# Gate logits in four column groups, turned back and added, in a fused attention, FFN and routed-experts kernel

## The chip, the cores and the metric

The kernel runs on one NeuronCore of a Trainium2 chip. The metric is the device time of one execution in microseconds, the median of three runs. The engines are TensorE (PE in the rows; PEld is its weight load, which runs beside the matmuls), VectorE (DVE), ScalarE (ACT), GpSimd (POOL) and SyncE (SP), which issues most transfers.

## The reference, cut to what matters

Three stages follow each other: clustered attention, a dense ELU feed-forward network, and a routed layer of eight experts. The change is in the routing of the third, for 1536 tokens of 512 numbers:

```python
skip_score = x @ w_skip
do_compute = skip_score > 0
xc = x[do_compute]
logits = xc @ w_gate                 # w_gate: 512 x 8
e_idx = np.argmax(logits, axis=1)
probs = softmax(logits); gate_w = probs[arange, e_idx]
for e in range(E):
    mask = e_idx == e
    h = np.maximum(xc[mask] @ w1[e], 0.0)
    y[mask] = gate_w[mask, None] * (h @ w2[e])
out[do_compute] = xc + y
```

## The kernel before

The tokens are two blocks of 768, each of six tiles of 128 tokens. The FFN runs over each block in 16 k-steps, one for each 128 of the hidden units. A k-step computes the hidden products of part 0 (three token tiles) into PSUM bank p and those of part 1 into bank v (`ffn_h`, L1275), passes each through the ELU (`ffn_elu`, L1295 to L1303: two ScalarE steps, a VectorE step, a ScalarE step and a VectorE step that all work on that bank or its copy), and then issues the 18 second products of the step before (`ffn_second`, L1314), which add into the other PSUM banks. All engines follow the program order in this stage.

Routing of a tile of 128 tokens has these steps. `turn` (T): four transposes into a bank (L1451) and a ScalarE copy of it to `x2T` (L1453). `logits` (L): four matmuls into a bank, each with 128 columns of `x2T` stationary and 16 columns of the gate table `wgs` moving (L1459; the 16 are eight gates, the skip weight and zeros), and a VectorE copy of the 128x16 result to `lg` (L1461). After the last tile of a half, `choose` (C, L1465 to L1478) finds each token's expert on VectorE and cumulates the counts in `cum`; `rank` (R) turns those into places with two small matmuls (L1482, L1483) and builds selections (L1486); `fill` (F) writes tokens and gate weights to slots (matmuls L1500, adds L1504).

Block 0 is routed beside the FFN of block 1. `route_beside` is a generator that `ffn` advances twice in each k-step: once after half of the second products (first slot) and once after the other half (second slot). Its order for each half of three tiles is T, L, T, L, T, L, one in each slot, then choose, an empty slot, rank, two empty slots, fill. Its banks come from one cycle over both halves:

```python
tags = itertools.cycle(("p", "v"))
halves = [self.route(b, 3 * half, y[half], lambda: self.ps(next(tags))[:, 0, :]) for half in range(2)]
```

Each call gives the next of the two banks; the tile that had the bank before must have been read.

Block 1 is routed in the tail, after its last k-step (`route_last`). TensorE's order there is the list `TAIL`, written out by hand. An h step is three of the second products that were held back (`h3` for tile 3, and so on); after the last of them for a tile that tile is copied out. `x-` and `x0` to `x5` gather the tokens of expert 0 with selections (L1537, matmuls L1541). `N5` (`ranks`, L1619) counts the tokens of each expert and gives the number of the next expert, with which its weights are fetched. The other engines' order in the tail is set by the scheduler, from the emitted program. The groups of the tail are tiles 0 to 2, 3 to 4, and 5 alone. Its banks rotate in the list `free`, which begins as p and v, loses v at `x-` and gains two more when the held products of tiles 4 and 5 are done.

Of the kernel before, what the change touches and what calls it, by code (L numbers as in the profile page):

```python
# [31 lines left out]
HOLD = 4  # L32


TAIL = ("h3 h3 h3 T0 T2 h3 L0 T1 h5 L2 L1 T3 h5 C0 h4 h4 R0 h4 h4 x- T4 h5 L3 L4 C3 h5 x0 T5 R3 x2 L5 x4 F0 C5 R5 N5 x3 x1 x5 F5 F3").split()

LATER = 8

# [125 lines left out]
class _Core:  # L164
# [75 lines left out]
    def constants(self):  # L240
        nc, c, E = self.nc, self.const, self.E
        V, S, G = nc.vector, nc.scalar, nc.gpsimd
        self.x2_d = self.dram.tile([self.NT, self.DM], F32, name="x2_d")
        self.wf_d = self.dram.tile([self.DFF // 128, 128, 1024], F32, name="wf_d")
        self.inv_d = self.dram.tile([self.B * self.H // 2, 12, 128], F32, name="inv_d")

        self.RS = (self.NT - min(WIDTHS) + 127) // 128 * 128
        self.meta_d = self.dram.tile([E * self.RS, 2], I32, name="meta_d")

        self.ones16 = c.tile([128, 128], BF16, name="ones16")  # L250
        V.memset(self.ones16, 1.0)
        self.tri16 = c.tile([128, 128], BF16, name="tri16")
        G.affine_select(out=self.tri16, in_=self.ones16, pattern=[[1, 128]], compare_op=ALU.is_gt,
                        fill=0.0, base=0, channel_multiplier=-1)

        io = c.tile([128, 16], I32, name="io")
        G.iota(io, pattern=[[1, 16]], base=0, channel_multiplier=0)
        self.iota16 = c.tile([128, 16], F32, name="iota16")
        V.tensor_copy(self.iota16, io)
        self.iota_neg = c.tile([128, 16], F32, name="iota_neg")  # L260
        V.tensor_scalar(self.iota_neg, self.iota16, -16.0, None, ALU.add)
        self.ebase = c.tile([128, E], F32, name="ebase")
        V.tensor_scalar(self.ebase, self.iota16[:, 0:E], float(self.RS), None, ALU.mult)
        self.tokid = c.tile([128, self.B, self.NC], I32, name="tokid")
        G.iota(self.tokid, pattern=[[self.S, self.B], [1, self.NC]], base=0, channel_multiplier=self.NC)
        io = self.pre.tile([128, CAP], I32, name="io_slot")
        G.iota(io, pattern=[[1, CAP]], base=0, channel_multiplier=0)
        self.iota_slot = c.tile([128, CAP], F32, name="iota_slot")
        V.tensor_copy(self.iota_slot, io)

        self.tok_neg = c.tile([128, self.B * self.NC], F32, name="tok_neg")
        V.tensor_scalar(self.tok_neg, self.tokid.rearrange("p b c -> p (b c)"), -NOWHERE, None, ALU.add)

        NTL = self.B * self.NC
        self.oh = c.tile([128, NTL, E], BF16, name="oh")
        self.pos = c.tile([128, NTL], F32, name="pos")
        self.gate = c.tile([128, NTL], F32, name="gate")

        self.slots = c.tile([SLOT, 2, E, 2], F32, name="slots")
        V.memset(self.slots, 0.0)  # L280

        self.oh_sc = c.tile([64, 2], F32, name="oh_sc")
        V.memset(self.oh_sc[0:32, 0:1], 1.0)
        V.memset(self.oh_sc[0:32, 1:2], 0.0)
        V.memset(self.oh_sc[32:64, 0:1], MASKED)
        V.memset(self.oh_sc[32:64, 1:2], -MASKED)
        self.sort_constants()
        self.top2 = c.tile([128, 1], I32, name="top2")
        V.memset(self.top2, -(1 << 30))

        self.acc = c.tile([128, E], BF16, name="acc")
        V.memset(self.acc, 0.0)


        self.wgs = c.tile([128, self.DM // 128, 16], F32, name="wgs")
        V.memset(self.wgs, 0.0)
        nc.sync.dma_start(out=self.wgs[:, :, 0:E], in_=self.w_gate.rearrange("(c p) e -> p c e", p=128))
        nc.sync.dma_start(out=self.wgs[:, :, E:E + 1], in_=self.w_skip.rearrange("(c p o) -> p c o", p=128, o=1))
# [732 lines left out]
    def redo_experts(self, d):  # L1031
# [9 lines left out]
        for i in range(T):  # L1041
            ps = self.ps("p")[:, 0, :]
            for c in range(4):
                PE.transpose(ps[:, c * 128:c * 128 + 128], out[:, i, c * 128:c * 128 + 128], self.ident)
            V.tensor_copy(xT[:, :, i * 128:i * 128 + 128], ps.rearrange("p (c n) -> p c n", c=4))
            ps = self.ps("v")[:, 0, 0:16]
            for c in range(4):
                PE.matmul(ps, lhsT=xT[:, c, i * 128:i * 128 + 128], rhs=self.wgs[:, c, :], start=(c == 0), stop=(c == 3))
            V.tensor_copy(lg[:, i], ps)
        ex, eq = t("ex", [128, T, E]), t("eq", [128, T, E])  # L1050
        V.tensor_reduce(st[:, 0], lg[:, :, 0:E], axis=AX.X, op=ALU.max)
# [271 lines left out]
    def second_ops(self, k):  # L1323

        NF = self.DFF // 128
        bl, f = divmod(k, NF)
        (w2H, w2L), g = self.w_sp[k, 1], [self.gs[k, part] for part in range(2)]

        def product(part, t, i):
            a, w = ((g[part][0], w2H), (g[part][1], w2H), (g[part][0], w2L))[i]  # L1330
            self.nc.tensor.matmul(self.y[bl][part][t], lhsT=a[:, t * 128:t * 128 + 128], rhs=w,  # L1331
                                  start=(f == 0 and i == 0), stop=(f == NF - 1 and i == 2))
        return product

# [85 lines left out]
    def route(self, b, c0, y, bank):  # L1420
# [32 lines left out]
            S.copy(held[t], ps)  # L1453

        def logits(t):
            lp = bank()[:, 0:16]
            x2T = held.pop(t)
            for j in range(4):
                PE.matmul(lp, lhsT=x2T[:, j * 128:j * 128 + 128], rhs=self.wgs[:, j, :],  # L1459
                          start=(j == 0), stop=(j == 3))  # L1460
            V.tensor_copy(lg[:, t, :], lp)  # L1461

        def choose():
            lge = lg[:, :, 0:E]
# [29 lines left out]
        def fill():  # L1494
# [7 lines left out]
            for g, n in enumerate((SLOT, CAP - SLOT)):  # L1502
                flat = self.slots[0:n, g].rearrange("p e v -> p (e v)")
                V.tensor_tensor(flat, ps[0:n, g * 2 * E:(g + 1) * 2 * E], flat, ALU.add)  # L1504
        return ([lambda t=t: copy(t) for t in range(nt)], [lambda t=t: turn(t) for t in range(nt)],
                [lambda t=t: logits(t) for t in range(nt)], choose, rank, fill)

    def first_fetch(self):

# [40 lines left out]
    def route_beside(self, b, y):  # L1550

        tags = itertools.cycle(("p", "v"))
        halves = [self.route(b, 3 * half, y[half], lambda: self.ps(next(tags))[:, 0, :]) for half in range(2)]
        for h in halves:
            for op in h[0]:
                op()
        yield
        for _, turn, logits, choose, rank, fill in halves:
            for i in range(3):
                turn[i]()  # L1560
                yield
                logits[i]()
                yield
            choose()
            yield
            yield
            rank()
            yield
            yield
            yield  # L1570
            fill()
            yield
        yield from self.first_fetch()

    def route_last(self, b, y, rest):

        self.oh0 = self.dp.tile([128, self.NC], F32, name="oh0")
        free, steps = ["p", "v"], {}

        def bank():  # L1580
            free.append(free.pop(0))
            return self.ps(free[-1])[:, 0, :]
        for c0, ys in ((0, y[0]), (3, y[1][0:2]), (5, y[1][2:3])):
            copy, turn, logits, choose, rank, fill = self.route(b, c0, ys, bank)
            for i in range(len(ys)):
                steps["c", c0 + i], steps["T", c0 + i], steps["L", c0 + i] = copy[i], turn[i], logits[i]
            steps["C", c0], steps["R", c0], steps["F", c0] = choose, rank, fill
        steps["N", 5] = lambda: self.ranks(bank)
        for c in range(3):
            steps["c", c]()  # L1590
        held = {c: [op for t, op in rest if t == c - 3] for c in range(3, 6)}
        with self.tc.manual_schedule(engines={mybir.EngineType.PE}):
            for what in TAIL:
                if what[0] == "h":
                    c = int(what[1])
                    held[c].pop(0)()
                    if not held[c]:
                        steps["c", c]()
                        if c > 3:
                            free.append(("sB", "t1")[c - 4])  # L1600
                elif what == "x-":
                    a = self.ps("sA")
                    self.xs_ps = [x[:, 0:WIDTHS[0]] for x in (a[:, 0, :], a[:, 1, :], self.ps("t0")[:, 0, :], self.ps("v")[:, 0, :])]
                    self.first_x(None)
                    free.remove("v")
                elif what[0] == "x":
                    self.first_x(int(what[1]))
                else:
                    steps[what[0], int(what[1])]()
        self.xs = {0: self.first_split()}  # L1610
# [366 lines left out]
```

## Time and profile before

| | us |
|---|---|
| median of 3 runs | 756.83 (756.13 to 759.34) |
| profiled execution | 756.85 |
| its span, first to last instruction | 755.1 |
| TensorE busy | 633.5 (84%) |
| VectorE busy | 429.9 (57%) |
| ScalarE busy | 392.4 (52%) |
| GpSimd busy | 272.8 (36%) |

TensorE is the busiest engine. Its busy time counts overlapping passes once, and the ends of matmuls are modelled, so the start-to-start distances of a timeline say more than the durations. An idle time in brackets in a timeline row stands before that row, with what ended it.

### The profile page before, as it was taken

The page shows a single profiled execution, that of the slowest core. Times are in us where ns is not written, and L with a number is a line of the kernel's source. Part 1 is how long each engine was busy: PE and PEld are TensorE (multiplying, and loading weights), DVE is VectorE, ACT ScalarE, POOL GpSimd, SP SyncE. Part 2 cuts the span into 40 slices and gives each one's busy share as a digit, 9 for nine tenths or more (in the row PEclk, how much of TensorE's full clock was granted, in tenths as well). Part 3 has the DMA queues.
Part 4 walks back from the last instruction along what each step waited for, and adds up shares of the span by engine and source line. Part 5 has one row for each costly group of instructions (what it writes and reads, how often), then busy time and mean ns, then how long its engine had stood idle before and what let it go on. Part 6 is the DMA issues. An engine that isn't in the chain of part 4 may idle for free.

```text
span 755.1 us, 11501 instructions
## 1 busy us (share of the span) xinstructions
PE 633.5 (84%) x3940; PEld 564.4 (75%) x3940; DVE 429.9 (57%) x978; ACT 392.4 (52%) x848; POOL 272.8 (36%) x289
## 2 busy tenths in 40 slices
PE   4882871984671399999999999999999998999996
PEld 2761761863561299978989888899998897999995
DVE  5681771883561298899788775243244554135663
ACT  3761750863640289776777765544444532124552
POOL 3237066047147302765664352323222203121101
PEclk9795795897695599999999999999999999999999
DMA  7867064566331029656655452642411037979960
GB/s 178 202 156 200 10 147 115 133 141 179 96 87 37 24 78 245 191 180 204 205 179 153 163 165 95 250 168 79 158 52 48 15 149 246 375 257 322 339 228 18
DMA packets 99958, 118.30 MB, mean 157 GB/s; under 512 B 47554, under 2 KB 68210, under 8 KB 99889
## 3 DMA queue, kind: packets, MB, share of 16 engines
q1 hardware_dynamic: 92080, 106.70, 46.4%
q0 software_dynamic: 6096, 10.34, 4.3%
q8 instruction: 33, 0.54, 0.3%
q10 hardware_dynamic: 1712, 0.43, 0.3%
q14 instruction: 37, 0.30, 0.1%
HBM read 80.17 MB, written 27.80 MB: 143 GB/s over the span
## 4 chain that ended last, share of the span: by engine, by line
PE 65%; DVE 13%; issue 10%; ACT 6%; another core or an unknown queue 5%; DMA 1%; ACTq 0%; POOL 0%; POOLq 0%; DVEq 0%
PE ps_p L1275 7%; PE ps_v L1275 6%; PE ps_t L1726 5%; PE ps_v L1741 4%; PE ps_p L1741 4%; PE ps_t L513 4%; PE ps_sB L1314 3%; PE ps_sA L1314 3%; PE ps_t L1314 3%; PE ps_v L544 3%; PE ps_sB L492 2%; DVE ptL L531 2%; DVE cv_b L1223 2%; PE ps_sA L1331 2%
## 5 line engine op out<-in xcount | busy, mean ns | idle before, releaser
L513 PE MATMUL ps_t<-ident,pe 128*128 128x128 f32 x288 | 54.1, 309 | 55.3 <-issue 29.9
L525 ACT ACTIVATE ptH<-ps_t 128x384 fp32r<-128x384 f32 x96 | 46.3, 493 | 89.3 <-remote 73.0
L531 DVE TENSOR_TENSOR ptL<-ps_t,ptH 128x384 fp32r<-128x384 f32 x96 | 52.1, 552 | 69.7 <-issue 54.7
L513 PEld LDWEIGHTS ps_t<-ident,pe 128*128 128x128 f32 x288 | 38.5, 158 | 65.8 <-issue 33.2
L874 POOL DMA_INDIRECT og<-od,idx x48 | 51.5, 1073 | 55.6 <-ACT rp L836 29.8
L544 PE MATMUL ps_v<-ptH,vt 128*128 128x256 f32 x144 | 43.4, 324 | 24.9 <-issue 12.4
L1229 POOL TENSOR_TENSOR r<-cv_b,cv_t 128x512 int32<-128x512 int32 x32 | 43.0, 1344 | 47.8 <-DVE cv_b L1223 17.7
L544 PEld LDWEIGHTS ps_v<-ptH,vt 128*128 128x128 f32 x144 | 30.1, 211 | 28.1 <-issue 14.4
L1774 POOL DMA_INDIRECT out_dram<-o,dest x10 | 11.5, 1151 | 96.0 <-DVE o L1772 95.4
L1275 PE MATMUL ps_p<-xH,w1H 128*128 128x384 f32 x128 | 44.3, 346 | 1.9 <-DVE gL L1303 1.4
L1275 PE MATMUL ps_v<-xH,w1H 128*128 128x384 f32 x124 | 42.0, 338 | 1.3 <-DVE gL L1303 1.3
L1299 DVE SCALAR_TENSOR_TENSOR ps_p<-e,ps_p 128x384 f32<-128x384 f32 x32 | 17.9, 561 | 44.0 <-ACT e L1297 44.0
L1275 PE MATMUL ps_p<-xL,w1H 128*128 128x384 f32 x128 | 43.0, 336 | 0.0
L1275 PE MATMUL ps_v<-xL,w1H 128*128 128x384 f32 x124 | 41.6, 335 | 0.0
L544 PE MATMUL ps_v<-ptL,vt 128*128 128x256 f32 x144 | 41.5, 312 | 0.0
L1255 POOL TENSOR_TENSOR w2L<-r,w2H 128x512 fp32r<-128x512 f32 x12 | 15.3, 1277 | 71.2 <-PE ps_t L1314 61.5
L1295 ACT ACTIVATE e<-ps_p 128x384 f32<-128x384 f32 x32 | 15.6, 488 | 40.7 <-PE ps_p L1275 40.5
L1741 PEld LDWEIGHTS ps_v<-xs,ew 128*128 128x128 f32 x256 | 34.6, 195 | 1.9
L1741 PE MATMUL ps_p<-xs,ew 128*128 128x128 f32 (+2 forms) x256 | 35.6, 281 | 0.5 <-ACT xs L1689 0.5
L1741 PE MATMUL ps_v<-xs,ew 128*128 128x128 f32 (+2 forms) x256 | 35.8, 284 | 0.0
L776 POOL DMA_INDIRECT kvs<-rowsH,idx x24 | 23.6, 984 | 33.5 <-DVE idx L754 26.8
L1741 PEld LDWEIGHTS ps_p<-xs,ew 128*128 128x128 f32 x256 | 33.8, 191 | 2.3 <-ACT xs L1689 0.6
(473 smaller groups left out, 1989.7 us busy)
## 6 DMA issues: line engine op xcount, KB each, us to landing
ew<-in_moe_w_dram SPq DMA_DIRECT2D x32, 1024.0 KB
d<-in_moe_w_in_dram SPq DMA_DIRECT2D x16, 512.0 KB
d<-in_moe_w_out_dram SPq DMA_DIRECT2D x16, 512.0 KB
wf_d<-r SPq DMA_DIRECT2D x16, 512.0 KB
r<-wf_d SPq DMA_DIRECT2D x16, 512.0 KB
zk<-kvs SPq DMA_DIRECT2D x8, 520.0 KB
KA<-kH SPq DMA_DIRECT2D x16, 192.0 KB
kvs<-zeros SPq DMA_DIRECT2D x8, 325.0 KB
```

Source lines behind the costliest of these rows:

```text
L513: self.nc.tensor.transpose(ps[:, 0, j * 128:j * 128 + 128], self.pe[u][:, half, j * 128:j * 128 + 128], self.ident)
L525: self.nc.scalar.activation(self.split(u, half)[0], self.tp[u, half][:, 0, 0:384].rearrange("p (c q) -> p c q", c=3), AF.Copy)
L531: self.nc.vector.tensor_tensor(l, self.tp.pop((u, half))[:, 0, 0:384].rearrange("p (c q) -> p c q", c=3), h.bitcast(F32), ALU.subtract)
L544: self.nc.tensor.matmul(self.vp[n, j], lhsT=self.vt[n][:, j // NG, c, :], rhs=t, start=(part == 0 and i == 0), stop=(part == 3 and i == 2 ...
L776: store = self.nc.gpsimd.indirect_dma_start(dst[2 * j + h], bass.IndirectOffsetOnAxis(ap=self.index(j, c, r), axis=0), self.sort_rows(j, c ...
L874: self.nc.gpsimd.indirect_dma_start(self.og[j][:, c, h, :], None, self.o_d[i], bass.IndirectOffsetOnAxis(ap=self.index(j, c, h), axis=0), ...
L1229: G.tensor_tensor(r[:, j * 512:j * 512 + 512].bitcast(I32), b, self.cvt.pop((f, j)), ALU.add)
L1275: self.nc.tensor.matmul(ps, lhsT=w[:, c, :], rhs=x[:, c, :], start=(i == 0), stop=(i == 11))
L1299: V.scalar_tensor_tensor(ps, e, -1.0, ps, ALU.add, ALU.max)
L1314: self.nc.tensor.matmul(self.y[bl][part][t], lhsT=a[:, t * 128:t * 128 + 128], rhs=w, start=(f == 0 and i == 0), stop=(f == NF - 1 and i = ...
L1726: PE.matmul(y[0][0:W], lhsT=a, rhs=b, start=(f == 0 and i == 0), stop=(f == NF - 1 and i == 2))
L1741: PE.matmul(ps[:, 0:W], lhsT=w1[:, c, i * 128:i * 128 + 128], rhs=xs[:, c, 0:W], start=(c == 0), stop=(c == 3))
```

## The change

The gate table is padded to 32 columns and becomes the stationary operand: the four matmuls of a tile write four groups of 32 PSUM partitions, one for each quarter of the 512 features, with 128 tokens moving. VectorE copies the 128x128 result to `lgT`; TensorE transposes that into columns 128 to 255 of a bank, and VectorE adds the four groups into `lg`. The transpose of a tile is issued behind the next tile's matmuls, in the same bank; that of a group's last tile is a step of its own, `back` (B in `TAIL`), which takes a bank. The group of one tile (tile 5) keeps the old form. `TAIL` is re-made, and `second_ops` looks up its operands later.

```diff
-TAIL = ("h3 h3 h3 T0 T2 h3 L0 T1 h5 L2 L1 T3 h5 C0 h4 h4 R0 h4 h4 x- T4 h5 L3 L4 C3 h5 x0 T5 R3 x2 L5 x4 F0 C5 R5 N5 x3 x1 x5 F5 F3").split()
+TAIL = ("h3 h3 h3 T0 T2 h3 L0 T1 h5 L2 h5 L1 T3 h4 B0 C0 h4 h4 R0 h4 x- T4 h5 L3 h5 L4 x0 B3 C3 T5 x2 R3 L5 x4 "
+        "F0 C5 R5 N5 x3 x1 x5 F5 F3").split()
...
-        self.wgs = c.tile([128, self.DM // 128, 16], F32, name="wgs")
+        self.wgs = c.tile([128, self.DM // 128, 32], F32, name="wgs")
...
-        (w2H, w2L), g = self.w_sp[k, 1], [self.gs[k, part] for part in range(2)]
+        w = self.w_sp[k, 1]
 
         def product(part, t, i):
-            a, w = ((g[part][0], w2H), (g[part][1], w2H), (g[part][0], w2L))[i]
-            self.nc.tensor.matmul(self.y[bl][part][t], lhsT=a[:, t * 128:t * 128 + 128], rhs=w,
+            a = self.gs[k, part][i % 2]
+            self.nc.tensor.matmul(self.y[bl][part][t], lhsT=a[:, t * 128:t * 128 + 128], rhs=w[i // 2],
                                   start=(f == 0 and i == 0), stop=(f == NF - 1 and i == 2))
...
         def logits(t):
-            lp = bank()[:, 0:16]
+            lp = bank()
             x2T = held.pop(t)
+            if nt == 1:
+                for j in range(4):
+                    PE.matmul(lp[:, 0:16], lhsT=x2T[:, j * 128:j * 128 + 128], rhs=self.wgs[:, j, 0:16],
+                              start=(j == 0), stop=(j == 3))
+                V.tensor_copy(lg[:, t, :], lp[:, 0:16])
+                return
             for j in range(4):
-                PE.matmul(lp, lhsT=x2T[:, j * 128:j * 128 + 128], rhs=self.wgs[:, j, :],
-                          start=(j == 0), stop=(j == 3))
-            V.tensor_copy(lg[:, t, :], lp)
+                PE.matmul(lp[32 * j:32 * j + 32, 0:128], lhsT=self.wgs[:, j, :], rhs=x2T[:, j * 128:j * 128 + 128],
+                          start=True, stop=True)
+            before = back(lp)
+            lgT = fw.tile([128, 128], F32, tag="lgT", bufs=2, name="lgT")
+            V.tensor_copy(lgT, lp[:, 0:128])
+            held["back"] = t, lgT
+            before()
+
+        def back(ps=None):
+            if "back" not in held:
+                return lambda: None
+            t, lgT = held.pop("back")
+            if ps is None:
+                ps = bank()
+            PE.transpose(ps[:, 128:256], lgT, self.ident)
+            add = lambda: V.tensor_reduce(lg[:, t, :], ps[:, 128:256].rearrange("p (j e) -> p e j", j=4)[:, 0:16, :], axis=AX.X, op=ALU.add)
+            return add
...
         return ([lambda t=t: copy(t) for t in range(nt)], [lambda t=t: turn(t) for t in range(nt)],
-                [lambda t=t: logits(t) for t in range(nt)], choose, rank, fill)
+                [lambda t=t: logits(t) for t in range(nt)], lambda: back()(), choose, rank, fill)
...
-        for _, turn, logits, choose, rank, fill in halves:
+        for _, turn, logits, back, choose, rank, fill in halves:
             for i in range(3):
                 turn[i]()
                 yield
                 logits[i]()
                 yield
+            back()
             choose()
...
+            steps["B", c0] = back
```

## Rows read from the trace of the kernel before

**Rows 1.** Busy time by stretch: stretch, its length, busy us (instructions) of each engine, clock, transfers.

```profile
500.00:590.00 90.00, 90.00 (x490) 81.91 (x489) 37.69 (x92) 43.35 (x87) 25.33 (x21) 1.00 0.23 77
```

**Rows 2.** Timeline around one turn and gate block of block 0: start, us, instruction.

```profile
529.83 0.49 ACT L1295 ACTIVATE e<-ps_v 128x384 f32<-128x384 f32 x1
...
531.72 0.60 PE L1451 MATMUL ps_p<-ident,xL 128*128 128x128 f32 x4
532.03 0.56 DVE L1303 TENSOR_TENSOR gL<-ps_v,gH 128x384 fp32r<-128x384 f32 x1 [0.56 <-ACT gH L1301]
532.08 0.48 PE L1314 MATMUL ps_sB<-w2H,gL 128*128 128x512 f32 x1
...
534.24 0.96 PE L1459 MATMUL ps_v<-wgs,x2T 128*128 128x16 f32 x8
535.05 0.42 PE L1275 MATMUL ps_p<-xH,w1H 128*128 128x384 f32 x1
```

**Rows 3.** Timeline at block 0's first rank and first fill.

```profile
513.88 0.19 PE L1482 MATMUL ps_p<-oh,tri 128*128 128x24 bf16 x1
514.19 0.56 DVE L1303 TENSOR_TENSOR gL<-ps_v,gH 128x384 fp32r<-128x384 f32 x1 [0.56 <-ACT gH L1301]
...
525.35 0.44 PE L1275 MATMUL ps_p<-xH,w1H 128*128 128x384 f32 x1
525.46 0.24 DVE L1504 TENSOR_TENSOR slots<-ps_v,slots 128x16 f32<-128x16 f32 x2 [2.23 <-PE ps_v L1500]
```

**Rows 4.** Timeline of TensorE around blocks in column groups in the sort.

```profile
40.45 0.34 PE L492 MATMUL ps_sA<-KA,QA 128*128 128x384 f32 x1
40.63 0.34 PE L492 MATMUL ps_sA<-KB,QB 80*128 80x384 f32 x1
40.89 0.85 PE L706 MATMUL ps_p<-sT,cwF 128*32 128x384 f32 x8
41.68 0.39 PE L544 MATMUL ps_v<-ptH,vt 128*128 128x256 f32 x1
...
151.54 0.49 PE L392 MATMUL ps_p<-qH,cwF 128*32 128x384 f32 x1
...
151.86 0.49 PE L392 MATMUL ps_p<-qL,cwF 128*32 128x384 f32 x1
```

**Rows 5.** Chain that ended last, in the tail and in expert 0.

```profile
609.03 0.89 PE ps_v L1459 x8
...
631.42 0.89 PE ps_p L1741 x8
```

**Rows 6.** Timeline of the tail.

```profile
609.96 0.17 DVE L1461 COPY lg<-ps_v 128x16 f32<-128x16 f32 x1 [0.72 <-PE ps_v L1459]
...
611.82 0.14 DVE L1478 TENSOR_TENSOR rcum<-rcum,oh 128x8 bf16<-128x8 bf16 x1
...
612.36 0.19 PE L1482 MATMUL ps_v<-oh,tri 128*128 128x24 bf16 x1
...
620.86 0.85 DVE L1537 TENSOR_SCALAR sel<-iota_slot,pos,oh 128x128 f32<-128x128 f32 x3
...
623.80 0.14 DVE L1478 TENSOR_TENSOR acc<-rcum,oh 128x8 bf16<-128x8 bf16 x1
...
623.99 0.17 PE L1619 MATMUL ps_t<-acc,ones 128*128 128x8 bf16 x1 [0.27 <-DVE acc L1478]
...
626.53 0.29 DVE L1547 COPY xs<-ps_sA 128x128 f32<-128x128 f32 x1 [0.15 <-PE ps_sA L1541]
```

**Rows 7.** Idle times of TensorE with the stretches behind them (timeline, busy time by stretch).

```profile
388.97 0.44 PE L1275 MATMUL ps_p<-xH,w1H 128*128 128x384 f32 x1 [1.02 <-DVE gL L1303]
388.00:392.00 4.00, 3.03 (x16) 2.90 (x17) 3.86 (x8) 2.55 (x6) 2.33 (x2) 1.00 0.59 228
638.93 0.49 PE L1726 MATMUL ps_t<-ew2HL,hH 128*128 128x512 f32 x1 [1.70 <-ACT hH L1744]
641.00:643.00 2.00, 2.00 (x8) 1.71 (x8) 0.29 (x1) 0.28 (x1) 0.00 (x0) 0.50 1.04 369
```

More of the change, by code (lines that the diff above doesn't have):

```diff
@@ L1047, in redo_experts @@
             for c in range(4):
-                PE.matmul(ps, lhsT=xT[:, c, i * 128:i * 128 + 128], rhs=self.wgs[:, c, :], start=(c == 0), stop=(c == 3))
+                PE.matmul(ps, lhsT=xT[:, c, i * 128:i * 128 + 128], rhs=self.wgs[:, c, 0:16], start=(c == 0), stop=(c == 3))
             V.tensor_copy(lg[:, i], ps)
@@ L1583, in route_last @@
         for c0, ys in ((0, y[0]), (3, y[1][0:2]), (5, y[1][2:3])):
-            copy, turn, logits, choose, rank, fill = self.route(b, c0, ys, bank)
+            copy, turn, logits, back, choose, rank, fill = self.route(b, c0, ys, bank)
             for i in range(len(ys)):
-                steps["c", c0 + i], steps["T", c0 + i], steps["L", c0 + i] = copy[i], turn[i], logits[i]
+                for x, f in zip("cTL", (copy, turn, logits)):
+                    steps[x, c0 + i] = f[i]
+            steps["B", c0] = back
             steps["C", c0], steps["R", c0], steps["F", c0] = choose, rank, fill
```

## The prediction, on record before the changed kernel ran

> **What bounds the kernel now.** I read the page's first part, then busy time by stretch, then the chain that ended last, then the timeline around every gate block. The profiled execution took 756.85 us (span 755.1) and the median of the three timed runs is 756.83, so a sum made against 756.85 carries over to the median as it is. A measurement of this kernel can tell about 0.5% (3.8 us) from no change.
>
> What counts are the two places of the gate. The first (block 0) lies inside the second FFN block, where TensorE is busy without a gap from 500 to 590 us [rows 1]: what it saves there is won in full, and each wait put into its queue is paid in full. The second (block 1) is the tail of routing, 604 to 628 us, where TensorE follows the written passage order, and the chain is TensorE nearly throughout, except where a rank or the number of the next expert needs a VectorE result.
>
> **The gate block itself.** Before, four matmuls are eight passes with 128 stationary columns. From the first pass to the next instruction of another kind it is 534.24 to 535.05, 0.81 us [rows 2], or 0.89 in the tail where another gate block stands before it [rows 5]. After, there are four column groups of 32. The trace has such blocks already, in the sort's similarities: eight passes of 128x32 with 384 moving columns take 0.85 us in all, and the next instruction starts 0.79 us after the first [rows 4]. In L392, which has the same form twice over, a round of four passes follows the other at 0.32 us [rows 4]. Four passes one after the other at that width would be 0.7 us even at the 0.18 us from start to start of L492, a lighter form, so the four groups of a round do overlap. Two rounds are 0.64 us, so 0.15 us are lost on the way out; on the way in, L492's pass would have given way at 40.63 + 0.18 = 40.81, and the block began at 40.89, so 0.08 us. With 128 columns a round is a third, 0.11 us: 0.08 + 2 x 0.11 + 0.15 = 0.45 us. The transpose back is a quarter of a turn's four, which take 532.08 - 531.72, 0.36 to 0.45 us, so 0.11 us. A block falls from 0.81 to 0.45 us, or to 0.56 us with a transpose: it saves 0.36 or 0.25 us.
>
> These rows give a factor of 1.8 at most. The Trainium skill, page TensorEngine Tiling (Array Packing), section When to Use Tiling, advises this very swap (narrow operand stationary, four column tiles), and its table of speedups names four as the ceiling. By that page a block would be an estimated 0.20 us, eleven blocks would give 6.7 us, the transposes would take back 1.2, and the time would be 751.4 us. The sum here keeps the row's 0.45 us.
>
> **Block 0, first half (tiles 0 to 2).** Three gate blocks save 0.36 + 0.25 + 0.25, the closing transpose costs 0.11: -0.75 us. That transpose stands a slot behind its copy, with half a step of products between, so it waits for nothing.
>
> **Block 0, what moves with it.** In route_beside the banks come from one cycle of p and v. A half takes eight so far (three turns, three gate blocks, rank, fill), so every turn and rank, which stand in the first slot of a k-step, get p, and every gate block and fill, in the second slot, get v. The FFN writes its hidden part 0 to p at the start of a step and part 1 to v behind it, so that pairing is free: at the first slot p has been read, and behind the second slot v isn't needed for a while. The closing back() takes a ninth bank. From there the pairing is reversed: rank of half 0 on v, its fill on p, three turns on v, three gate blocks on p, the closing transpose of half 1 on v. Its rank and fill are in step again.
>
> A first-slot bank on v must wait until ELU part 1 has read v. Its last reader is L1303, ending 532.03 + 0.56 = 532.59, and the turn stands at 531.72 [rows 2]. With 0.05 us from VectorE to TensorE (acc ends 623.94, TensorE goes on at 623.99 [rows 6]) that is a wait of 0.92 us. At the rank it is 514.19 + 0.56 + 0.05 - 513.88 = 0.92 us [rows 3]. The three turns and the closing transpose repeat the pattern: five waits, 4.6 us. Everything behind them on TensorE (the other half of the second products, then the next step) waits too, and nothing later can take it back, since TensorE has no idle time there. The ELU can't come earlier: its first step starts 529.83, as soon as part 1 is there and part 0 has left ScalarE.
>
> A second-slot bank on p must be read before the next step's first product writes p. For fill that is L1504, ending 525.70, plus 0.05, against 525.35: 0.40 us [rows 3]. For a gate block: passes end about 0.50 us after the slot, 0.04 us to VectorE, a 128x128 copy out of PSUM 0.29 us [rows 6], 0.05 us back: 0.88 against 0.81, +0.07 us. With the sum behind the copy (0.2 us, an estimate between the 0.14 us of an add of 8 columns and that copy's 0.29 us [rows 6]) 1.08: +0.27, twice. The trace doesn't show whether the copy must let the transpose into the same bank finish first; that would be 0 to 0.17 us more for each, and I take 0, as the copy can start when the passes are done. Half 1 in all: 4.6 + 0.11 + 0.40 + 0.61 = +5.7 us. Block 0: **+5.0 us**.
>
> **Block 1, the tail.** Five gate blocks are replaced (tile 5 keeps its form): 0.36 + 0.25 + 0.33 before the first rank, 0.36 + 0.33 before the second, less 0.11 each for the closing transposes. Against that stand two longer ways to a rank. Before, choose starts from the copy right behind the last gate block, and the cumulated counts are there 1.83 us after that copy ends (610.13 to 611.96), ahead of TensorE's coming to the rank at 612.36 [rows 6]. After, the way is copy, transpose, sum, choose. The order covers the copy (a turn and an h step), but the sum is ready 0.4 us after the transpose has left TensorE, the counts 1.83 us later, and only two h steps, 1.4 us (0.70 us each in the chain), stand before the rank: a wait of 0.8 us. That is all that was saved up to there. For the second rank the same: about 1.6 us for two tiles, and T5 and x2 before it, 1.3 to 1.4 us: a wait of 0.6 us. Besides, the second rank now stands behind x2 (0.89 us, eight passes of 128 columns as in rows 5), where it stood ahead of it. So the selections for x4, which were finished at 620.86 + 0.85 when x4 began [rows 6], have only L5 as cover: x4 waits 0.4 to 1.0 us, and L5's copy can stand behind the selections on VectorE, with rank 5 and the choice of the next experts (623.99) behind it. I take **+0.7 us**; it is -0.8 us if none of these waits comes, +1.2 us if all do. All h steps are still issued, and the rewritten second_ops issues the same products in the same order: nothing. The wider gate table is a constant of the start, and TensorE's first use of it is hundreds of microseconds later: nothing; without that cover, one somewhat larger memset.
>
> Sum: 756.85 + 5.0 + 0.7 = **762.5 us**, +0.75%. Its own range is 760.3 to 764.5 us.
>
> **Rivals.**
> *The wrong bank costs nothing* (the other side). If ELU part 1 ended 0.9 us before the slot, the five waits would vanish, and with them the reason for slower. Then 2 x -0.75 for block 0, and between -0.8 and +0.7 in the tail: 754 to 756.5 us, down to 751.4 with the ceiling named above. It decides at the end of L1303 against the first slot; the rows have it 0.9 us late. 0.12.
> *Part of the waits is given back.* The reads of p are quicker and the tail keeps its savings: 757.5 to 760 us. 0.12.
> *The clock falls at the new waits.* It was at 0.50, the 1.2 GHz level, in the 2 us from 641 on, behind an idle of 1.70 us, so at least 1 us was lost [rows 7]. Against it: after an idle of 1.02 us in the FFN it stayed at 1.00 [rows 7], and the waits here are 0.9 us. One to five such falls would be +1 to +5, and more if they last longer: 764 to 771 us. 0.08.
> *The groups run one after the other.* Eight passes of 128 columns are 0.89 us [rows 5], so a block would cost 1.2 us instead of 0.56: 767 to 770 us. Rows 4 speak against it. 0.06.
>
> **How the numbers follow.** My forecast has 0.62. The range 756.5 to 767 leaves out most of the first rival (0.10) and the upper part of the last two (0.08). Slower by over 0.5% (above 760.6): 0.60 + 0.08 + 0.06 + 0.02 from the second rival's edge = 0.76. Within 0.5%: 0.19. Faster: 0.05.
>
> **What the profile would show.** Right: in the second half of block 0's gate (520 to 570 us) turns on ps_v that wait about 0.9 us for L1303, and first products on ps_p that wait for a VectorE copy or sum; gate blocks of 128x32 of about 0.45 us; a first rank of the tail that waits for the counts. Wrong: turns still on ps_p, or on ps_v with no idle time before them; a tail from its first turn to expert 0 that is shorter than before; blocks of 0.8 us and more; a clock below 1.00 between 500 and 600 us.

## The result and the profile after

The changed kernel takes 764.28 us (median of 6 runs, 762.31 to 766.75) against 756.53 us for the kernel before, measured beside it: a ratio of 1.0098, with a 95% interval of 1.0073 to 1.0124. By that ratio it is slower by 7.4 us (the medians differ by 7.75); forecast were 762.5 us and a range of 756.5 to 767. A second comparison (after_again, below) gives 1.0086 [1.0061, 1.0112].

The profiled execution after took 764.43 us (span 762.71), 7.58 us more in span than the one of before. Landmarks that both traces have, here the start of TensorE's first turn of each block, the start of the first product of expert 0 and the end, cut the spans into four stages:

```
                                      before    after    difference
start to first turn of block 0        476.53   478.82    +2.29
block 0 (to first turn of the tail)   127.76   133.99    +6.23
tail (to expert 0)                     23.65    24.34    +0.69
expert 0 to the end                   127.19   125.56    -1.63
```

In the first and the last stage nothing was changed but the width of the gate table, and their differences are taken as those of two executions: the last stage took 127.11 us in after_again, the same kernel, and the first 474.35 us in bank_back, which has every edit of the change up to there. What is the change's own is then +6.92 us. The windows of the trace after, for the stretch of [rows 1] and for block 0 and the tail whole (columns as there):

```profile
500.00:590.00 90.00, 84.14 (x463) 72.83 (x462) 34.76 (x89) 39.50 (x79) 25.64 (x20) 1.00 0.25 82
478.82:612.81 133.99, 127.49 (x695) 110.75 (x693) 52.30 (x125) 62.87 (x127) 35.60 (x28) 1.00 0.28 95
612.81:637.15 24.34, 22.89 (x191) 18.10 (x191) 15.10 (x95) 6.23 (x14) 0.00 (x0) 1.00 0.32 131
```

TensorE, busy for all of the 90 us before, is now idle for 5.86 us of them. The clock stays at 1.00. In these 90 us TensorE sits idle nine times, in the places that the forecast named. The timeline at the first rank, at its fill, around one turn and gate block of the second half, and at a gate block that carries a transpose (it answers to [rows 2, 3]):

```profile
516.02 0.56 DVE L1304 TENSOR_TENSOR gL<-ps_v,gH 128x384 fp32r<-128x384 f32 x1 [0.56 <-ACT gH L1302]
516.63 0.17 PE L1503 MATMUL ps_v<-oh,tri 128*128 128x24 bf16 x1 [0.76 <-DVE gL L1304]
...
528.18 0.24 DVE L1525 TENSOR_TENSOR slots<-ps_p,slots 128x16 f32<-128x16 f32 x2 [2.24 <-PE ps_p L1521]
528.57 0.41 PE L1276 MATMUL ps_p<-xH,w1H 128*128 128x384 f32 x1 [0.43 <-DVE slots L1525]
...
535.24 0.56 DVE L1304 TENSOR_TENSOR gL<-ps_v,gH 128x384 fp32r<-128x384 f32 x1 [0.56 <-ACT gH L1302]
535.85 0.66 PE L1452 MATMUL ps_v<-ident,xL 128*128 128x128 f32 x4 [0.76 <-DVE gL L1304]
...
538.50 0.43 PE L1466 MATMUL ps_p<-x2T,wgs 128*32 128x128 f32 x8
538.99 0.29 DVE L1470 COPY lgT<-ps_p 128x128 f32<-128x128 f32 x1 [3.19 <-PE ps_p L1466]
539.34 0.44 PE L1276 MATMUL ps_p<-xH,w1H 128*128 128x384 f32 x1 [0.41 <-DVE lgT L1470]
...
549.26 0.43 PE L1466 MATMUL ps_p<-x2T,wgs 128*32 128x128 f32 x8
549.62 0.33 PE L1480 MATMUL ps_p<-ident,lgT 128*128 128x128 f32 x1
549.99 0.29 DVE L1470 COPY lgT<-ps_p 128x128 f32<-128x128 f32 x1 [3.42 <-PE ps_p L1480]
550.20 0.22 DVE L1481 TENSOR_REDUCE lg<-ps_p 128x16 f32<-128x64 f32 x1
550.56 0.41 PE L1276 MATMUL ps_p<-xH,w1H 128*128 128x384 f32 x1 [0.61 <-DVE lg L1481]
```

How to read it: the rank, the turns and the closing transpose are now on ps_v and start 0.05 us after the end of L1304, the last reader of that bank. The 0.76 us in brackets is counted from the modelled end of the matmul ahead; from where the instruction would have started it is 0.92 us, since the pass ahead, started at 515.48, gives way after 0.23, at 515.71. There are five such waits (the others at 535.85, 546.62, 557.84 and 569.05), and four first products on ps_p that wait for a VectorE copy, sum or add (528.57, 539.34, 550.56, 561.78). The last group shows what the second kind hangs on: the copy waits for the transpose into the same bank, and the next product for the sum behind the copy.

The gate block itself, in the first half where its bank is v and nothing waits, and the tail's waits (they answer to [rows 2] and [rows 6]):

```profile
481.42 0.43 PE L1466 MATMUL ps_v<-x2T,wgs 128*32 128x128 f32 x8
481.77 0.44 PE L1276 MATMUL ps_p<-xH,w1H 128*128 128x384 f32 x1
...
621.19 0.19 PE L1503 MATMUL ps_p<-oh,tri 128*128 128x24 bf16 x1 [0.22 <-DVE oh L1493]
621.63 0.17 PE L1504 MATMUL ps_p<-rcum,ones 128*128 128x24 bf16 x1 [0.25 <-DVE rcum L1499]
...
628.43 0.39 PE L1562 MATMUL ps_v<-sel,xH 128*128 128x128 f32 x2
629.05 0.18 PE L1503 MATMUL ps_p<-oh,tri 128*128 128x16 bf16 x1 [0.24 <-DVE oh L1493]
629.26 0.17 PE L1504 MATMUL ps_p<-rcum,ones 128*128 128x16 bf16 x1
629.29 1.04 PE L1461 MATMUL ps_sB<-wgs,x2T 128*128 128x16 f32 x8
630.71 0.71 PE L1562 MATMUL ps_sA<-sel,xL 128*128 128x128 f32 x4 [0.37 <-DVE sel L1558]
...
633.20 0.17 PE L1643 MATMUL ps_sB<-acc,ones 128*128 128x8 bf16 x1 [0.33 <-DVE acc L1499]
```

The block is 0.35 us from its first pass to the next product, and about 0.09 us goes ahead of it (the pass before started at 481.10 and a pass of that kind gives way after 0.23): 0.44 us where it was 0.81, as costed. The brackets of the tail's rows, too, count from modelled ends; what these waits cost from start to start is worked out further down.

### The profile page after: what moved, and what is told of

Same layout as the page of the kernel before. It is cut to its first block, busy times and chain, and to the rows that moved or that the text cites. A ratio compares the mean times of both kernels' runs of the same rounds, so it can differ in the third digit from the quotient of the medians.

```text
span 762.7 us, 11532 instructions
## 1 busy us (share of the span) xinstructions
PE 630.3 (83%) x3951; PEld 554.7 (73%) x3951; DVE 432.8 (57%) x989; ACT 391.8 (51%) x848; POOL 272.1 (36%) x289
## 4 chain that ended last, share of the span: by engine, by line
PE 55%; DVE 16%; ACT 9%; another core or an unknown queue 9%; issue 6%; DMA 4%; POOL 0%; SPq 0%; ACTq 0%; POOLq 0%; DVEq 0%
PE ps_p L1276 5%; PE ps_t L1750 4%; PE ps_v L1765 4%; PE ps_p L1765 4%; PE ps_v L1276 4%; PE ps_t L514 3%; PE ps_v L545 3%; PE ps_t L1315 2%; DMA r<-wf_d 2%; PE ps_sB L1315 2%; PE ps_sA L1315 2%; DVE ptL L532 2%; DVE cv_b L1224 2%; ACT pe L506 2%
```

## The experiments

The theory: the closing transpose takes a ninth bank, this reverses the pairing of slots and banks for the rest of block 0, and the waits behind that are the loss; column groups alone are a gain of about half a block each. The first rival: the loss lies in the column groups, their transposes and sums, whatever the bank. The second: it lies in the re-made tail. Two numbers are read from each profile: the block-0 stretch (first turn to first turn of the tail; 127.76 before, 133.99 after) and the tail up to N5, the count that gives the next expert (19.70 before, 20.39 after). Ratios are to the kernel before on the same chip; its median was 757.13 us for the first four runs and 757.67 for the next three that were timed.

**bank_only.** The kernel before, with a bank passed over and nothing else:

```diff
                 logits[i]()
                 yield
+            next(tags)
             choose()
```

> The kernel before, with nothing but one bank of route_beside's cycle passed over behind each half's third gate block. No column groups, no transposes back. Theory (reversed banks): rank of the first half and three turns of the second wait 0.92 us each on ps_v, the first fill and three gate blocks are waited for 0.4 us each on ps_p: the stretch from block 0's first turn to the tail's first turn goes from 127.8 to about 133.1, the time to about 761.8. Rival (groups and transposes): no change, 756.5.

Measured: 761.08 us, 1.0059 [1.0032, 1.0086]; stretch 133.38 us, tail to N5 19.70 us. Its timeline, TensorE's waits in the first rank, its fill, and one turn and gate block:

```profile
515.07 0.17 PE L1482 MATMUL ps_v<-oh,tri 128*128 128x24 bf16 x1 [0.77 <-DVE gL L1303]
...
527.01 0.41 PE L1275 MATMUL ps_p<-xH,w1H 128*128 128x384 f32 x1 [0.42 <-DVE slots L1504]
534.29 0.66 PE L1451 MATMUL ps_v<-ident,xL 128*128 128x128 f32 x4 [0.77 <-DVE gL L1303]
538.08 0.45 PE L1275 MATMUL ps_p<-xH,w1H 128*128 128x384 f32 x1 [0.27 <-DVE lg L1461]
```

One line that issues no instruction costs +5.62 us of the stretch (about 133.1 us were expected), with the old gate blocks. The waits need no column groups.

**bank_back.** The changed kernel with the pairing set right again:

```diff
             back()
+            next(tags)
             choose()
```

> The changed kernel, with one bank of route_beside's cycle passed over behind each closing transpose, so that rank and fill, and all of the second half, are on the banks of before. Theory (reversed banks): the five waits of 0.9 us on ps_v and the four reads of ps_p go; from block 0's first turn to the tail's first turn 127.3 us (134.0 in the changed kernel, 127.8 before), and the time falls from 764.3 to 757 to 757.7. Rival (the column groups and the transposes cost it themselves, in drains and in the bank they share with the copy): that stretch stays at 133 or more and the time at 763 or more.

Measured: 756.89 us, 0.9999 [0.9970, 1.0028]; stretch 126.65 us, 7.34 us under after; tail to N5 20.41 us, as in after. The first rank is on ps_p again and no instruction waits; TensorE's busy time in the stretch of [rows 1]:

```profile
511.25 0.19 PE L1503 MATMUL ps_p<-oh,tri 128*128 128x24 bf16 x1
```

```profile
500.00:590.00 90.00, 90.00 (x494) 80.08 (x493) 39.99 (x99) 44.95 (x90) 26.72 (x21) 1.00 0.23 76
```

Both ends of the theory hold: the bank alone makes a loss of that size, and without it the stretch is 1.11 us better than before. The transposes, sums and copies of the new form are all still there, so the first rival falls.

**block0_only** and **tail_only.** The new form in one place alone, the other with its old form and, for block0_only, its old order; block0_only with the bank passed over as in bank_back:

```diff
-            if nt == 1:
+            if nt == 1 or b:          # block0_only; tail_only: nt == 1 or b == 0
```

> Column groups in block 0 alone, on the banks of before (one of the cycle passed over behind each closing transpose); the tail has the form and the order of before. Theory: block 0 saves 0.5 us in its first half, where one step is held by a weight transfer, and 0.7 in its second: 126.6 us from its first turn to the tail's; the tail 23.65 us as before; 755.3 us. Rival (groups cost it themselves): 128 us or more, 757 or more.

> Column groups and the re-made order in the tail alone; block 0 keeps the old form, and so its banks. Theory: the tail, from its first turn to expert 0's first product, goes from 23.65 to 24.3 us by the waits at the two ranks and at x4; block 0 as before; 757.2 us. Rival (the tail gains what its gate blocks save, and the waits are covered): 22.5 us, 755.4.

Measured: block0_only 754.76 us, 0.9977 [0.9942, 1.0012], stretch 126.68, tail to N5 19.70. tail_only 756.44 us, 0.9982 [0.9953, 1.0011], stretch 127.72, tail to N5 20.31. By stage the two places add up: the tail's loss (+0.61) is there without block 0's change, block 0's gain (-1.08) without the tail's. So the second rival holds for 0.6 to 0.7 us, and for no more. Neither total differs measurably from before. tail_only's way from N5 to expert 0 was 6.63 us where before has 3.95: in its window TensorE is at half its clock (the eighth column, 0.50: 1.2 GHz of 2.4), with no idle time and 35 passes in 6 us.

```profile
624.00:630.00 6.00, 6.00 (x35) 5.92 (x35) 4.73 (x34) 0.03 (x1) 0.00 (x0) 0.50 0.06 5
```

So the 24.3 us that were expected up to expert 0 did not come (26.94), and that is why the tail is read up to N5. block0_only has such a stretch there too (5.58 us from N5 to expert 0).

**one_group.** bank_back, with the quarters accumulated in one group of 32 partitions instead of four groups, so that the four matmuls follow each other in the same 32 columns; the copy is 32x128 and the sum a copy:

```diff
-                PE.matmul(lp[32 * j:32 * j + 32, 0:128], ...)
-                          start=True, stop=True)
+                PE.matmul(lp[0:32, 0:128], ...)
+                          start=(j == 0), stop=(j == 3))
```

> The changed kernel on the banks of before, but the four quarters of the features go one after the other into one group of 32 columns and are added there by TensorE; the copy has 32 partitions, the turned-back result is copied instead of summed. Theory (the four groups of a round run at once): a gate block of 1.0 us and more instead of 0.35 to 0.43, so about 0.6 us more for each of six tiles: from block 0's first turn to the tail's 130.2 us (126.65 with groups on the same banks), the time 759 to 761. Rival (the narrow stationary operand alone makes the block short): 126.7 us, 757.

Measured: 764.16 us, 1.0081 [1.0054, 1.0109]; stretch 131.18 us, +4.53 us over bank_back for six blocks of block 0. The timeline of one block:

```profile
479.82 1.06 PE L1466 MATMUL ps_v<-x2T,wgs 128*32 128x128 f32 x8
480.81 0.44 PE L1276 MATMUL ps_p<-xH,w1H 128*128 128x384 f32 x1
```

It is 0.99 us to the next product, against 0.35 with four groups. So the groups do overlap in the changed kernel, which is what the forecast's fourth rival denied. The stretch is 1.0 us over the 130.2 expected; of the 4.53 us, six blocks at 0.64 us more make 3.9, and the rest was not traced. The time lies over the expected 759 to 761 us, which left out the tail's five blocks: its way to N5 is 24.13 us, 3.72 us over bank_back's.

**turn_first.** The changed kernel with `before = back(lp)` ahead of the four matmuls, so that the transpose is not what the copy waits for; it was run and profiled once.

> The changed kernel, banks as it has them, with the transpose back of the tile before issued ahead of the four column-group matmuls instead of behind them. Theory (the VectorE copy waits for the last TensorE instruction in its bank, which is the transpose): the copy starts behind the matmuls, some 0.15 us earlier, so from the second to the third turn of block 0's second half 11.05 us instead of 11.22. Rival (the copy waits for the matmuls alone, and something else holds the bank): 11.2 us or more.

Measured: 763.67 us in its one profiled run; the step between the second and the third turn of the second half 11.10 us (after 11.22, before 9.66). The timeline of that gate block:

```profile
558.50 0.27 PE L1480 MATMUL ps_p<-ident,lgT 128*128 128x128 f32 x1
558.70 0.43 PE L1467 MATMUL ps_p<-x2T,wgs 128*32 128x128 f32 x8
559.19 0.29 DVE L1470 COPY lgT<-ps_p 128x128 f32<-128x128 f32 x1 [3.34 <-PE ps_p L1467]
559.40 0.21 DVE L1481 TENSOR_REDUCE lg<-ps_p 128x16 f32<-128x64 f32 x1
559.76 0.41 PE L1276 MATMUL ps_p<-xH,w1H 128*128 128x384 f32 x1 [0.64 <-DVE lg L1481]
```

The copy now waits for the matmuls, 0.49 us behind their first pass, but against the first pass of the whole block it comes hardly earlier (0.69 us, 0.73 in after): in either order it begins when both passes and transpose are done. Only 0.12 us of the expected 0.17 is won at this step, and none over the stretch (134.02 us; 133.99 in after); the tail to N5 is longer, 20.84 us. The price of the block on p is the sequence matmuls, transpose, copy, sum, one after the other.

**more_cover** and **cover_all.** bank_back with the tail re-ordered once more: x1 ahead of x4 and N5, and the first rank behind x- (more_cover), or behind one more h step and x- (cover_all):

```diff
-    ... T3 h4 B0 C0 h4 h4 R0 h4 x- T4 ... R3 L5 x4 F0 C5 R5 N5 x3 x1 x5 F5 F3     # after
+    ... T3 h4 B0 C0 h4 h4 x- R0 h4 T4 ... R3 L5 x1 x4 F0 C5 R5 N5 x3 x5 F5 F3     # more_cover
+    ... T3 h4 B0 C0 h4 h4 h4 x- R0 T4 ... R3 L5 x1 x4 F0 C5 R5 N5 x3 x5 F5 F3     # cover_all
```

> The changed kernel on the banks of before, and in the tail x- put ahead of the first rank and x1 ahead of x4, so that more TensorE work stands between a transpose back and the rank that needs its sums, and between the second rank and x4. Theory (the tail pays for the way over the transpose back because too little work covers it): the waits of 0.47 us at the first rank, 0.37 at x4 and 0.33 before the count of tokens go, from the tail's first turn to expert 0 23.2 us at full clock (24.34 in the changed kernel); 755.8 us. Rival (the waits only move on to the next instruction that needs a VectorE result): 24 us or more, 757.

> As the run with more cover, with the last h4 ahead of x- and the first rank, so that the copy of tile 4 has x- as cover too (there T4 waited 0.68 us for it). Theory (each wait of the tail is the way to a VectorE or ScalarE result with too little TensorE work in between): from the tail's first turn to expert 0 23.1 us at full clock instead of 23.8, block 0 126.65, the time 754. Rival (the saved wait comes back at the next instruction): 23.7 us.

Measured: more_cover 754.67 us, 0.9955 [0.9930, 0.9979]; tail to expert 0 23.78 us (23.2 expected; before 23.65), to N5 20.36 with x1 ahead of it. The waits at the first rank, at x4 and at N5 are gone, a wait of 0.25 us came at x5, without a bracket, and one that was not expected for ScalarE's copy of tile 4, since the last h4 now stands right ahead of T4:

```profile
613.00 0.66 PE L1452 MATMUL ps_p<-ident,xL 128*128 128x128 f32 x4 [0.68 <-ACT xL L1443]
```

cover_all removes that one too: the tail is 22.84 us to expert 0, better than before, and 19.43 to N5, which now has x1 (0.89 us) ahead of it. Yet its total, on a chip where the kernel before takes 751.37 us, is 751.47: 0.9999 [0.9978, 1.0020].

Both ran again, each a second time, side by side on one chip:

> The kernel of more_cover a second time, beside cover_all_2 on one chip. If the stages set the time: block 0 126.6 us as before in more_cover, the tail 23.8 us, and a time 1.1 us under the kernel before (ratio 0.9985), so that most of the 0.9955 of the first comparison was scatter. If the first comparison was a real gain that the stages do not show, the ratio is 0.9955 again.

> The kernel of cover_all a second time, on the same chip as more_cover_2. If the stages set the time: block 0 126.6 us, the tail 22.8 us, 1.9 us under the kernel before (ratio 0.9975) and 0.9 us under more_cover_2, unless the stall at the hidden products of expert 0 takes it back as in cover_all (an idle time of over 2 us there again: ratio 0.998 to 1.000). If that stall is of the one execution, it is under 1.7 us here and the gain shows.

Measured: 647.43 us, 0.9986 [0.9959, 1.0012], and 649.12 us, 0.9997 [0.9977, 1.0018]; the kernel before took 648.16 us there. The stages of both come out as in their first profiles within 0.02 us (block 0 126.66, tail 23.77 and 22.84). So the 0.9955 of more_cover did not come again, and cover_all's 1.9 us by stage (1.12 in block 0, 0.81 in the tail) is twice not found in the total. In its second profile the experts' stage is 127.10 us, 3.28 us longer than that of more_cover_2. There TensorE stops for 2.76 us, from 556.08 to 558.84, until ScalarE's activation L1773 is done, and ScalarE waits for a transfer of expert weights (timeline of ScalarE; window of all engines, the last two columns are the transfers' busy share and GB/s):

```profile
557.46 0.63 ACT L1729 ACTIVATE ew2HL<-ew 128x512 fp32r<-128x512 f32 x1 [5.12 <-DMA ew<-in_moe_w_dram]
558.00 0.61 ACT L1729 ACTIVATE ew2H<-ew 128x512 fp32r<-128x512 f32 x1
558.52 0.27 ACT L1773 ACTIVATE h<-ps_p 128x144 f32<-128x144 f32 x1
```

```profile
550.00:560.00 10.00, 7.24 (x52) 7.02 (x51) 1.88 (x4) 3.01 (x8) 0.00 (x0) 0.91 1.04 386
```

The weight split L1729 stands ahead of the activation L1773 on ScalarE, and all transfer engines are busy. From the end of the stop to 561.6 us TensorE's granted clock is 0.50, which costs up to 1.4 us more. Where the gain goes is shown here for one execution; in cover_all's first profile the stall is 2.40 us, at another place of the same stage (632.85, ScalarE's L1769), and what held ScalarE there the trace does not name. No version was shown to beat the kernel before.

**after_again.** The changed kernel unaltered, to see which differences between profiles repeat:

> The changed kernel once more. Theory: of the 7.6 us between the two profiles, the 2.3 us before block 0's first turn and the 1.6 us the other way behind expert 0's start are not the change's: they come out otherwise here, while the stretch from block 0's first turn to the tail's is 134.0 us again, and the tail to the count of tokens 20.4. Rival (the change moves what lies before and behind the gate too): 478.8 us to block 0's first turn, and 125.6 from expert 0 on.

Measured: 765.20 us, 1.0086 [1.0061, 1.0112]. Block 0 134.07 us and tail to N5 20.40, as in the first profile (133.99, 20.39); start to block 0 480.53 us (478.82), expert 0 to the end 127.11 us (125.56). The outer stages move by 1.5 us and more between executions of one kernel, the two inner ones by less than 0.1 us.

## Why the forecast was right, and where its numbers were off

**The mechanism held.** Forecast were +5.0 us in block 0 and +0.7 us in the tail; measured were +6.23 and +0.69. bank_only and bank_back show the cause from both sides. Of the 7.4 us of the timed runs the forecast has 5.7; most of what is missing lies in block 0.

**The five first-slot waits** were costed at 0.92 us each from the end of L1303 against the slot, and are 0.92 us each. The fill's wait was costed at 0.40 us; from the rank to the first turn of the second half, which holds it and that turn's own wait, the way is 19.22 us against 17.84 before, +1.38 where 0.40 + 0.92 = 1.32 was costed.

**The term that was mis-sized: gate blocks on p.** The steps of the second half came out 1.10, 1.56 and 1.73 us longer, forecast from its terms 0.99, 1.19 and 1.30. The forecast asked whether the copy must let the transpose into the same bank finish first and took nothing for it, 0.17 us at most. As the program stands, it must: in the rows above, the copy at 549.99 stands 0.73 us behind the first pass and waits for the transpose at 549.62; without a transpose it stands 0.49 us behind (538.50, 538.99). The block costs 549.18 to 550.56, 1.38 us, not 1.08 (549.18 is when the pass ahead gives way). Two such blocks are 0.60 us, half of the 1.2 us that block 0 was mis-sized by. turn_first shows that the order of the two in the bank hardly matters.

**The first half saved less:** 0.46 us and not 0.75. The first block's saving is partly taken back at the next turn. In the trace after, the ELU of part 0 is late in that step, since ScalarE's split of weights waits for their transfer; the idle time is 3.98 us there, the same as before:

```profile
485.06 0.63 ACT L1247 ACTIVATE w1H<-r 128x512 fp32r<-128x512 f32 x1 [3.98 <-DMA r<-wf_d]
```

```profile
487.78 0.56 DVE L1304 TENSOR_TENSOR gL<-ps_p,gH 128x384 fp32r<-128x384 f32 x1 [0.56 <-ACT gH L1302]
...
488.39 0.66 PE L1452 MATMUL ps_p<-ident,xH 128*128 128x128 f32 x4
```

The turn follows L1304's end (488.34) at 0.05 us, where the pass before it, started at 487.92, gives way at 488.15: 0.24 us lost with no bracket to show it, because that pass is modelled to last longer. Before, the same turn was 0.04 us late. The half of bank_back that has no such transfer (its second) saves 0.66 us. The rest of the 1.2 us, some 0.3 us, is spread over the other steps and was not traced.

**The tail** came out as forecast, in sum and nearly term by term, once its waits are counted from start to start like those of block 0. The first rank is late by 0.39 us (from where the last h pass gives way, 620.57 + 0.23), and its second matmul, which needs the counts, by 0.40 us more: 0.8, as forecast. The second rank follows x2 0.39 us late (628.43 + 0.23 against 629.05), and L5 follows the rank after 0.24 us where x2 did so after 0.05 before:

```profile
619.75 0.17 PE L1482 MATMUL ps_p<-oh,tri 128*128 128x16 bf16 x1
...
619.80 0.69 PE L1541 MATMUL ps_sA<-sel,xH 128*128 128x128 f32 x4
```

That is 0.58 us, forecast 0.6; the bracket of 0.24 us shows less than half of it. L5 would give way to x4 after 0.89 us [rows 5], at 630.18, and x4 starts at 630.71: 0.53 us, within the forecast 0.4 to 1.0. N5 waits 0.07 us longer than before. Together that is 1.97 us, so what the blocks save, less their transposes, must be 1.97 - 0.69 = 1.28 us. cover_all bears this out: it is 0.81 us ahead of before at expert 0, with the second rank's 0.58 us and a wait of 0.25 at x5 left (621.77 + 0.23 against 622.25), and without N5's wait, 0.40 us in before from start to start; so 1.24 us are saved in work. The forecast's terms for the same work add up to 1.41 us. Its figure of -0.8 us for a tail without any of these waits does not follow from them (that would be -1.4), but the +0.7 does.

**The rivals.** "The wrong bank costs nothing" is refuted by L1304's end at each slot. "Part of the waits is given back" did not happen either: each of the five first-slot waits has its full 0.92 us. "The clock falls at the new waits" did not come: nine waits of 0.4 to 0.8 us by the brackets, and 1.00 in the window. "The groups run one after the other" is refuted by the 0.35 us of the block and by one_group. With the ceiling of four that the Trainium skill, page TensorEngine Tiling (Array Packing), section Theoretical Speedup, gives, a block would be an estimated 0.20 us; measured is 0.44, a factor of 1.8, and even with the bank set right block 0 gains 1.1 us for six blocks. The same page, section PSUM Bottleneck, says that tiling does not speed up the reading of PSUM and that the copy may become the limit; the trace agrees (the copy of the 128x128 result takes 0.29 us where the 128x16 one took 0.17 [rows 6], and a sum of 0.22 us is added), and on a bank that the next product needs at once it decides: a block on p loses 0.12 us without a transpose (0.93) and 0.57 with one (1.38) against the old form on v. The old form on p, in bank_only, costs 1.23 us, from 536.85 to 538.08.

**The profiles' own scatter.** The sum of the change is +6.92 us, the spans differ by 7.58. The other +2.29 and -1.63 us lie in stages without any change. The second fits the half-speed stretch of [rows 7], which the trace after does not have: 3.4 us at half the clock cost up to 1.7 us. after_again, which has such a stretch there, takes 127.11 us from expert 0 on, bank_only, which has none, 125.5.

## What to carry to other kernels

When several users draw banks in turn from one cycle, count the draws: an extra one flips which bank every later user meets, and the loss comes in places that the edit does not touch. A cheap test of such a theory is to add the draw alone to the old kernel and to take it out of the new one. In a stretch where one engine is busy throughout, compare by landmarks inside the stretch: they repeat within 0.1 us, where whole executions differ by 2 us or more. Count a wait of TensorE from start to start and against a place where nothing waits: the idle time in brackets is counted from a modelled end, and here it showed 0.16 us less than the wait, or no wait at all.

## What was not expected

**The clock.** Half-speed stretches of TensorE (granted clock 0.50) in the tail and the experts come and go between profiles of nearly the same instructions. Two of them stand behind a stop for ScalarE in expert 0: in before (640.5 to 643.9 us) behind 1.70 us, in after_again (650.4 to 653.8) behind 1.86 us. The trace after has that stop too and keeps its clock at 1.00 (timeline, and the window behind it):

```profile
648.13 0.49 PE L1750 MATMUL ps_t<-ew2HL,hH 128*128 128x512 f32 x1 [1.69 <-ACT hH L1768]
648.00:652.00 4.00, 3.87 (x25) 3.40 (x25) 1.48 (x4) 1.32 (x5) 0.00 (x0) 1.00 1.04 362
```

bank_only (1.73 us) and cover_all (2.40 us) also have the stop and no such stretch. So the fall behind an idle of 1.70 us, from which the forecast's third rival took its price, does not come each time. In five other profiles the clock falls late in the tail, while TensorE is busy and no bracket in the 12 us ahead is over 0.38 us: bank_back from 621.4 us, block0_only from 626.8, tail_only from 623.8, turn_first from 630.1 and one_group from 631.1, for 3.4 us in the first two and 6.8 us in the others. The tail of after has the same waits and no fall. The nine new waits of block 0 caused none. What sets these stretches stays open.

**The stage before the FFN.** On the last chip (more_cover_2, cover_all_2) all three kernels took some 100 us less; by the two profiles taken there all of it lies ahead of block 0 (371 us against 475). TensorE's waits in that stage, for cover_all on one chip and then for cover_all_2 on the other (what waited, for what; us in total, times, longest):

```profile
PE ps_t L514 <- issue: 38.7, 8, 11.1
PE ps_t L514 <- DVE ptL L532: 22.2, 8, 9.5
PE ps_v L545 <- DVE xr L562: 8.4, 1, 8.4
```

```profile
PE ps_t L514 <- DVE ptL L532: 2.0, 4, 0.6
```

The long stops, "issue" among them (no event of the profile ends them), are absent on that chip. TensorE's granted clock differs with them: 0.79 over the first 300 us of cover_all, 0.97 over the first 200 us of cover_all_2. The gate's two stages are the same on both within 0.02 us, so nothing said above hangs on it; its cause was not looked for.
